# Half-width cluster choice in the opening, products summed in PSUM in the later first layers, and late weight sums on VectorE in a fused attention and MLP kernel

## The chip, the cores and the metric

The kernel runs on one core of a Trainium2 chip. The metric is the device time of one execution in microseconds (us). The core has a TensorE for matrix products (PE in the profile, with its weight loads apart as PEld), a VectorE (DVE), a ScalarE (ACT), a GpSimd (POOL) and a SyncE (SP), whose queue here issues nearly all DMAs. Each engine works through its own queue in order, and semaphores make one engine wait for another. SBUF is the on-chip memory of 128 partitions; PSUM is the small memory of eight banks that TensorE writes its products to and can add them up in.

## The reference, cut to what matters

```python
# attention: B=4, H=8 heads, S=768, D=64, 16 clusters
q_assign = argmax(q_n @ c_n^T)          # per head; k_assign alike
mask     = q_assign[:, None] == k_assign[None, :]
scores   = where(mask, q @ k^T / 8, -1e9)
attn     = softmax(scores)
x        = attn @ v                      # then (B, H, S, D) -> (3072, 512)
# MLP: w_in 512 x 2048, w_out 2048 x 512 (given as 64-bit floats)
h = x @ w_in
g = h / (1 + exp(-1.702 * h))
out = g @ w_out
```

A query attends only to the keys of its own cluster. All sums are made in fp32. The weights come as 64-bit floats, and the kernel rounds them to 32 bits itself.

## The kernel before, in words

**Attention.** Two heads form a pair, and there are 16 pairs. A pair is worked in 12 units: two halves of the queries, six tiles of 128 keys each. The loop over `t` does two units per turn. For a unit, `scores` makes the transposed scores (keys on partitions, 384 queries along the row) in PSUM, `part` adds the mask as a second product into the same bank, `exps` takes the exponential on ScalarE, `add_up` adds the exponentials into the denominators (on GpSimd, in halves of 384; the first sum of every even group on VectorE), and one turn later `values` multiplies with v. After every third turn `row_sums_of` sums over the partitions with a product, and `normalise` divides on VectorE.

The mask of the first pair is made from one-hot rows: `prep_turn` transposes q and k of pair 0 with TensorE, `prep_near` scores them against the centroids, `prep_assign` finds the best centroid on VectorE and writes a one-hot tile `hot`, and `prep_hot` transposes it into `hots0` and `hots1`, which `part` multiplies. The later pairs go through two rows of codes in DRAM instead (`prep_spread`). The preparation of pair p + 1 is spread over the turns of pair p.

`rounding` converts one chunk of 512 weights per partition, in five steps on VectorE, with the help of a PSUM bank. There are 32 chunks. `step` does one step, and a list of turns says where five steps (a whole chunk) are done. A chunk also issues the load of the chunk two places on. `keep_busy(n)` issues n products of an identity matrix that nobody reads (fillers) into the tile `idle`.

**MLP.** For each of the four batches a first and a second layer follow. The first layer is cut into 2x2 blocks and uses seven products per block of outputs in place of eight. `first7` does this for one of eight values of `f`: each product is a pair of contractions of 128 into a PSUM bank, and VectorE adds of a bank and the tile `G` combine the products (seven adds, one copy on ScalarE). `finish` is the activation, on ScalarE. The operands of the products are sums of blocks of x (`sums_x`, tiles Tx2 to Tx4, on VectorE) and of w_in (`sums_w`, on GpSimd).

The second layer uses two levels of this, 49 products in seven steps `k`: `second49(k, ...)` does the seven products of one step and already adds products up in PSUM banks x and v. Its operands are sums of G (`sums_t`, `sums_G`, on VectorE, in tiles E0 to E2, Tx2 to Tx4, Y and G itself) and sums of w_out (tile Wz, three per step). In batch 0 `keep_w` makes the Wz sums on GpSimd and stores them in DRAM, and the later batches load them. Those of steps 5 and 6 are made late, inside the second layer of batch 0, by `load_sums(k, made=True)`. After each step the result is added into the Y tiles, on GpSimd except for steps 4 and 5 (`i in (5, 7)`) of the last batch. While a second layer runs, VectorE also makes the next batch's `sums_x` and turns finished outputs for their stores (`store`).

The order of each queue is the order in which the program is written (manual scheduling): nothing is moved by a scheduler.

Of the kernel before, what the change touches and what calls it, by code (L numbers as in the profile page):

```python
# [8 lines left out]
FP32 = mybir.dt.float32  # L9
# [29 lines left out]
def fast(  # L39
# [31 lines left out]
    P = 128  # L71
# [44 lines left out]
    def short():  # L116
        return tmp.tile([P, HALF], FP32, name="short")
# [180 lines left out]
                rhs=ident_h[:, None, :].broadcast_to((P, 4, P)),  # L298
                start=True, stop=True)

    keep_busy(6)
    cps = bank()
    nc.tensor.transpose(out=cps[:, 0:P], in_=cc.rearrange("p a d -> p (a d)"),
                        identity=ident)
# [62 lines left out]

    def prep_assign(p):
        ps = bank()
        if p > 0:  # L370
            nc.vector.transpose(out=ps[:, 0:HALF], in_=sT.pop(p)[:, 0:HALF])
        else:
            for n in range(NH):
                nc.tensor.transpose(out=ps[:, n * P:(n + 1) * P],
                                    in_=sT[p][:, n * P:(n + 1) * P],
                                    identity=ident)
# [4 lines left out]
        eq = sc if p > 0 else short().bitcast(BF16)[:, 0:n * NC].rearrange(  # L381
            "p (n c) -> p n c", c=NC)
# [7 lines left out]
        if p == 0:  # L390
            code[p] = asg.tile([P, n], FP32, name="code", bufs=1)
            nc.vector.tensor_reduce(out=code[p], in_=eq, axis=AX.X,
                                    op=ALU.max)
            nc.vector.tensor_tensor(
                out=hot[:, :, 0:NC],
                in0=code[p][:, :, None].broadcast_to((P, n, NC)),
                in1=rank[:, None, :].broadcast_to((P, n, NC)),
                op=ALU.is_equal)
            return
        nc.vector.tensor_reduce(  # L400
            out=codes[:, 0:n].rearrange("p (w a j) -> p w j a", a=2, j=NJ),
            in_=eq.rearrange("p (w j a) c -> p w j a c", a=2, j=NJ),
            axis=AX.X, op=ALU.max)
        turned = ps[:, HALF:HALF + SQ]
        nc.vector.transpose(out=turned, in_=codes)
        row = code[p] = asg.tile([P, 2, SQ], BF16, name="row")
        nc.vector.tensor_copy(out=row[:, 0], in_=turned)
        nc.vector.scalar_tensor_tensor(
            out=row[:, 1], in0=turned, scalar=1.0 / CODE, in1=row[:, 0],
            op0=ALU.mult, op1=ALU.mult)  # L410
# [14 lines left out]
                    in_=line[b, at:at + NJ, :].rearrange(  # L425
                        "j t -> (j t)")[None, :])

    def prep_hot(p):


        rows = slice(0, 2 * SQ)
        for w in range(2):
            hots[w] = hp1.tile([P, S], BF16, name=f"hots{w}")
            ps = bank().bitcast(BF16)
            for h in range(2):
                for n in range(NH):
                    at = (h * NH + n) * P
                    nc.tensor.transpose(
                        out=ps[rows, at:at + P],
                        in_=hot_w(w, h, n), identity=ident_h)  # L440
            dst = hots[w][rows, :]
            if w == 0:
                nc.vector.tensor_copy(out=dst, in_=ps[rows, 0:S])
            else:
                nc.scalar.activation(out=dst, in_=ps[rows, 0:S], func=AF.Copy,
                                     scale=FAR, bias=-FAR)
# [6 lines left out]
    PREP += [prep_near, prep_assign,  # L453
             lambda p: (prep_hot if p == 0 else prep_spread)(p)]

# [202 lines left out]

    steps = (0, 0, 0, 5, 0, 5)
    made = sums_x(0)
    for p, i in [(0, i) for i in range(6)] + [(1, i) for i in range(2)]:
        prep(p, i)
        if p == 0 and i in (1, 3):
            load_w(i // 2)
        if (p, i) == (0, 4):
            keep_busy(3)
    for t in range(NT + 2):
        us = range(2 * t, 2 * t + 2) if t < NT else ()  # L670
        for u in us:
            scores(u)
        if t == 0:
            keep_busy(6)
            prep(0, 6)
            keep_busy(4)
        for u in us:
            part(u)
        for u in us:
            exps(u)  # L680
# [12 lines left out]
        while later:  # L693
            later.pop()()
        if 1 <= t <= NT:
            for u in range(2 * t - 2, 2 * t):
                values(u)
        if t >= 2 and (t - 2) % TG == TG - 1:
            row_sums_of((t - 2) // TG)
        while work and PREP[work[0][1]] == prep_near:  # L700
            prep(*work.pop(0))
        if t >= NT - 8 and t < NT:
            XT = list(next(made))
        for p, i in work:
            prep(p, i)
        for _ in range(0 if t in (0, 1, 2, NT - 1) else 5 if t == 4 else
                       steps[t % (2 * TG)]):
            step()
        if tests and t % (2 * TG) in (1, 2, 3, 5):
            tests.popleft()()  # L710
        if t >= 2 and (t - 2) % TG == TG - 1:
            normalise((t - 2) // TG)
# [70 lines left out]

    def spare_y():
# [62 lines left out]
    def first7(b, f, X, T):  # L847
# [31 lines left out]
        add(g1[:, 0], p, g1[:, 0])  # L879
        finish(g2[:, 0])  # L880
        finish(g1[:, 0])

    def after7(f):

# [142 lines left out]
    pend = iter(())  # L1027
    for b in range(B):
        for f in range(FB):
            first7(b, f, *XT)  # L1030
            sums_w(b * FB + f + 2)
            if f:
                after7(f - 1)
# [43 lines left out]
        for k in range(7):  # L1077
# [461 lines left out]
```

## Time and profile before

| | us |
|---|---|
| median of three runs | 901.17 (900.03 to 901.57) |
| the profiled execution's own time | 900.34 |
| span of its instructions | 898.5 |
| TensorE busy in the span | 885.8 |
| VectorE busy | 728.3 |
| GpSimd busy | 497.4 |
| ScalarE busy | 366.1 |

The span runs from the first to the last instruction that the profiler recorded; all positions below are microseconds from its start. By TensorE's timeline the first scores start at 11.44, attention ends at about 342, and then first and second layers alternate: 342 to 414 and 414 to 481 for batch 0, and so on to 891. A row of the profile names line, engine, operation, output and inputs, shape and count; what stands in brackets is the idle time of the engine just before and what ended it.

### The profile page before, as it was taken

How to read it: one execution, taken by the hardware profiler on the slowest of the kernel's cores; microseconds unless marked ns; L12 is line 12 of the kernel's file. 1: busy time of each engine (PE TensorE's matmuls, PEld its weight loads, DVE VectorE, ACT ScalarE, POOL GpSimd, SP SyncE). 2: the span in 40 equal slices, each digit the busy share in tenths (PEclk: the TensorE clock that was granted, in tenths of full speed). 3: DMA queues.
4: the chain of work that ended last, by engine and by line, in shares of the span. 5: the costliest groups of instructions: out<-in, count | busy, mean ns of one | idle time of the engine just before them, and what ended most of it. 6: DMA issues, size and time to landing. Idle time of an engine off the chain costs nothing.

```text
span 898.5 us, 17781 instructions
## 1 busy us (share of the span) xinstructions
PE 885.8 (99%) x6720; PEld 581.4 (65%) x6720; DVE 728.3 (81%) x1183; ACT 366.1 (41%) x819; POOL 497.4 (55%) x469
## 2 busy tenths in 40 slices
PE   8999999999999999999999999999999999999997
PEld 3444444444444445558996557998556998556996
DVE  4999989999999997998998556798556798556795
ACT  3677767777677764322111232111232111222111
POOL 5899999998999998693274221143121134120130
PEclk9999999999999999999999999999999999999999
DMA  9566556666575310036113202223202223200224
GB/s 175 122 129 112 103 120 130 143 143 133 133 139 119 85 43 19 0 122 230 71 54 107 52 1 71 84 74 107 53 1 70 73 76 117 43 10 0 71 71 109
DMA packets 176333, 78.97 MB, mean 88 GB/s; under 512 B 152824, under 2 KB 159472, under 8 KB 176240
## 3 DMA queue, kind: packets, MB, share of 16 engines
q1 hardware_dynamic: 175984, 77.63, 35.2%
q8 instruction: 55, 0.90, 0.4%
q14 instruction: 38, 0.31, 0.1%
q10 hardware_dynamic: 256, 0.13, 0.1%
HBM read 61.03 MB, written 16.70 MB: 87 GB/s over the span
## 4 chain that ended last, share of the span: by engine, by line
PE 87%; DVE 8%; issue 2%; POOL 1%; DMA 1%; ACT 0%; SPq 0%; DVEq 0%; ACTq 0%; POOLq 0%
PE b L854 32%; PE b L904 23%; PE s L472 13%; PE o L537 12%; PE s L495 3%; PE m L554 3%; DVE G L598 2%; DVE E L598 2%; POOL sum L521 1%; PE m L348 1%; DVE Tx L598 1%; DMA in<-in_k_dram 1%; DVE x L598 0%; DVE e L200 0%; DVE y L845 0%
## 5 line engine op out<-in xcount | busy, mean ns | idle before, releaser
L521 POOL TENSOR_TENSOR sum<-sum,A 128x384 f32<-128x384 f32 x252 | 265.5, 1091 | 25.7 <-ACT A L503 16.6
L845 DVE TENSOR_TENSOR G<-b,G 128x384 f32<-128x384 f32 x224 | 123.1, 556 | 98.7 <-PE b L854 89.5
L503 ACT ACTIVATE A<-s 128x768 f32<-128x768 f32 x192 | 146.3, 809 | 91.1 <-PE s L495 71.0
L598 POOL TENSOR_TENSOR Y<-y,Y 128x768 f32<-128x768 f32 x28 | 67.4, 2421 | 175.0 <-DVE y L845 151.0
L859 ACT ACTIVATE G<-G 128x384 f32<-128x384 f32 x128 | 66.3, 523 | 199.1 <-DVE G L845 197.7
L472 PE MATMUL s<-T,T 64*64 64x384 f32 x1536 | 142.9, 487 | 0.7 <-ACT A L503 0.7
L537 PE MATMUL o<-A,inv 64*64 64x384 f32 x1536 | 141.2, 483 | 0.0
L598 POOL TENSOR_TENSOR W<-w_in 128x256 f32<-128x256 f32 x32 | 23.6, 737 | 163.8 <-PE b L854 163.5
L598 DVE TENSOR_TENSOR G<-G 128x768 f32<-128x768 f32 (+1 forms) x92 | 104.5, 1159 | 0.0
L472 PEld LDWEIGHTS s<-T,T 64*64 64x64 f32 x1536 | 54.9, 132 | 70.1 <-ACT A L503 36.4
L854 PE MATMUL b<-x,W 128*128 128x384 f32 x256 | 93.1, 486 | 0.0
L854 PE MATMUL b<-Tx,w_in 128*128 128x384 f32 x256 | 93.1, 486 | 0.0
L854 PE MATMUL b<-x,w_in 128*128 128x384 f32 x256 | 88.6, 486 | 0.0
L537 PEld LDWEIGHTS o<-A,inv 64*64 64x64 f32 x1536 | 58.3, 133 | 38.5 <-issue 33.5
L854 PEld LDWEIGHTS b<-x,W 128*128 128x128 f32 x256 | 48.6, 190 | 33.9
L854 PEld LDWEIGHTS b<-Tx,w_in 128*128 128x128 f32 x256 | 48.6, 190 | 33.9
L854 PEld LDWEIGHTS b<-x,w_in 128*128 128x128 f32 x256 | 48.5, 190 | 33.5 <-issue 0.6
L904 PE MATMUL b<-G,w_out 128*128 128x192 f32 x320 | 55.9, 326 | 0.0
L904 PEld LDWEIGHTS b<-G,w_out 128*128 128x128 f32 x320 | 52.7, 190 | 1.1
L904 PE MATMUL b<-E,Wz 128*128 128x192 f32 x288 | 51.5, 328 | 1.4 <-DVE E L598 1.4
L904 PEld LDWEIGHTS b<-E,Wz 128*128 128x128 f32 x288 | 47.1, 190 | 3.4 <-POOL Wz L598 1.3
L854 PE MATMUL b<-Tx,W 128*128 128x384 f32 x128 | 46.6, 487 | 1.5 <-DVE Tx L598 1.5
(169 smaller groups left out, 1366.4 us busy)
## 6 DMA issues: line engine op xcount, KB each, us to landing
Wz<-kept_w SPq DMA_DIRECT2D x78, 256.0 KB
raw<-in_moe_w_in_dram SPq DMA_DIRECT2D x16, 512.0 KB
raw<-in_moe_w_out_dram SPq DMA_DIRECT2D x16, 512.0 KB
inv<-in_v_dram SPq DMA_DIRECT2D x16, 384.0 KB
in<-in_q_dram SPq DMA_DIRECT2D x60, 96.0 KB
in<-in_k_dram SPq DMA_DIRECT2D x60, 96.0 KB
kept<-x SPq DMA_DIRECT2D x24, 192.0 KB
x<-kept SPq DMA_DIRECT2D x24, 192.0 KB
```

What stands on the lines that cost most here:

```text
L348: nc.tensor.matmul(out=ps[r:r + SQ, w * NJ * SQ:(w + 1) * NJ * SQ] .rearrange("p (j t) -> p j t", t=SQ), lhsT=cT[:, p % HP].rearrange("p a ...
L472: nc.tensor.matmul(out=ps[c:c + D, a, 0:HALF], lhsT=T[p, 1][rows, kt * P + c:kt * P + c + D], rhs=T[p, 0][rows, h * HALF:(h + 1) * HALF], ...
L495: nc.tensor.matmul(out=s_of[u][c:c + D, a, :], lhsT=rows_of[1, p % 2][rows, kt * P + c:kt * P + c + D], rhs=rows_of[0, p % 2][rows, h * HA ...
L503: nc.scalar.activation(out=A_of[u], in_=s_of.pop(u), func=AF.Exp, scale=SCALE)
L521: nc.gpsimd.tensor_tensor(out=sum_of[g][:, a], in0=(A_of[u - 1] if kt == 1 else sum_of[g])[:, a], in1=A_of[u][:, a], op=ALU.add)
L537: nc.tensor.matmul(out=o_of[g][a * D:(a + 1) * D, r, 0:HALF], lhsT=v_in[p][rows, a, kt, :], rhs=A[rows, a, :], start=(kt == 0), stop=(kt = ...
L554: nc.tensor.matmul(out=ps[a * D:(a + 1) * D, 0:HALF], lhsT=twos, rhs=sm[:, a, :], start=(i == 0), stop=(i == len(parts) - 1))
L598: engine.tensor_tensor(out=o, in0=a, in1=b, op=(ALU.add if op == "+" else ALU.subtract))
L845: nc.vector.tensor_tensor(out=o, in0=p, in1=a, op=ALU.add)
L854: nc.tensor.matmul(out=ps[:, 0:HALF], lhsT=a[:, c], rhs=x(c), start=(c == 0), stop=(c == 1))
L859: nc.scalar.activation(out=g, in_=g, func=AF.Gelu_apprx_sigmoid, scale=2.0)
L904: nc.tensor.matmul(out=ps, lhsT=A[n][:, f], rhs=M[n][:, f], start=start and f == 0, stop=(f == FQ - 1), skip_group_check=True)
```

## The change

It has four parts.

- **The opening.** `prep_assign` and `prep_hot` of pair 0 become two halves of the tokens: `first_turns` does the transposes, the generator `choice(h)` does the five VectorE operations for one half, and `prep_hot(h)` transposes one half and copies it into half of `hots0` and `hots1`. For w = 0 the transposes go to the second bank of `idle`. Unit 2 gets its `part` and `exps` ahead of the scores of unit 3, and the second half of the one-hot work stands between them. The q and k turns of pair 1 on VectorE come after the second half's choice. The fillers change from 6, 3, 6 and 4 to 8, 2, 1, 3 and 3, the last three behind the first `part`.
- **The rounding chunks.** Turn t = 5 does none any more, and turn t = 91 (NT - 5), in the last pair, does one.
- **PSUM sums.** For batches 1 to 3 a new `first7_psum` takes the place of `first7`. It uses three banks per f, lets TensorE add four of the seven products into them, and leaves three VectorE adds and three ScalarE copies. One activation reads PSUM directly.
- **Late sums on VectorE.** The Wz sums made inside batch 0's second layer, and the Y sums of steps 4 and 5 of batch 0, go to VectorE.

```diff
-    keep_busy(6)
+    keep_busy(8)
...
+    def first_turns(p):
+        first.append(bank())
+        for n in range(NH):
+            nc.tensor.transpose(out=first[0][:, n * P:(n + 1) * P], in_=sT[p][:, n * P:(n + 1) * P], identity=ident)
...
+    def choice(h):
+        n = NJ * 2
+        ps, eq = first
...
+        nc.vector.tensor_reduce(out=best.rearrange("p (n a) -> p n a", a=2), in_=sc, axis=AX.X, op=ALU.max)
+        yield
+        nc.vector.tensor_tensor(out=eq4, in0=sc, in1=..., op=ALU.is_equal)
+        nc.vector.tensor_tensor(out=eq[:, h], in0=eq[:, h], in1=ranks, op=ALU.mult)
+        nc.vector.tensor_reduce(out=of, in_=eq[:, h], axis=AX.X, op=ALU.max)
+        nc.vector.tensor_tensor(out=hot..., in0=of..., in1=rank..., op=ALU.is_equal)
+        yield
...
+    def prep_hot(h):
+        rows, cols = slice(0, 2 * SQ), slice(h * HALF, (h + 1) * HALF)
+        pss = idle[:, 1, :].bitcast(BF16), bank().bitcast(BF16)
+        for w in (1, 0):
+            for n in range(NH):
+                nc.tensor.transpose(out=pss[w][rows, n * P:(n + 1) * P], in_=hot_w(w, h, n), identity=ident_h)
+        nc.scalar.activation(out=hots[1][rows, cols], in_=pss[1][rows, 0:HALF], func=AF.Copy, scale=FAR, bias=-FAR)
+        nc.vector.tensor_copy(out=hots[0][rows, cols], in_=pss[0][rows, 0:HALF])
...
         if (p, i) == (0, 4):
-            keep_busy(3)
+            keep_busy(2)
+    halves = [choice(h) for h in range(2)]
+    for h in (0, 0, 1):
+        next(halves[h])
     for t in range(NT + 2):
...
             scores(u)
+            if u == 2:
+                part(u)
+                exps(u)
+                prep_hot(1)
         if t == 0:
-            keep_busy(6)
-            prep(0, 6)
-            keep_busy(4)
+            keep_busy(1)
+            prep_hot(0)
+            keep_busy(3)
+            next(halves[1])
+            for i in range(2):
+                prep(1, i)
         for u in us:
-            part(u)
+            if u != 2:
+                part(u)
+        if t == 0:
+            keep_busy(3)
...
-        for _ in range(0 if t in (0, 1, 2, NT - 1) else 5 if t == 4 else
-                       steps[t % (2 * TG)]):
+        for _ in range(0 if t in (0, 1, 2, 5, NT - 1) else
+                       5 if t in (4, NT - 5) else steps[t % (2 * TG)]):
             step()
...
-    def keep_w(k, o):
+    def keep_w(k, o, engine=nc.gpsimd):
...
-            sums(nc.gpsimd, ((o, x, op, z),))
+            sums(engine, ((o, x, op, z),))
...
-            keep_w(k, [W[k][:, i] for i in range(3)])
+            keep_w(k, [W[k][:, i] for i in range(3)], nc.vector)
...
+    def first7_psum(b, f, X, T):
...
+        g1, g2 = G[:, f], G[:, f + FB]
+        x, z, v = (bank_b() for _ in range(3))
+        product(x, A_in(0, 0, f), lambda c: X[0, 0, c])
+        nc.scalar.copy(g1[:, 0], x)
+        product(z, A_in(0, 1, f), lambda c: X[1, 0, c])
+        add(g1[:, 0], z, g1[:, 0])
+        product(x, S[2], lambda c: T[2, c], False)
+        nc.scalar.copy(g1[:, 1], x)
+        finish(g1[:, 0])
+        product(v, S[1], lambda c: T[1, c])
+        nc.scalar.copy(g2[:, 1], v)
+        product(x, S[3], lambda c: T[3, c], False)
+        add(g2[:, 1], x, g2[:, 1])
+        finish(g2[:, 1])
+        product(v, S[4], lambda c: X[1, 1, c], False)
+        add(g1[:, 1], v, g1[:, 1])
+        finish(g1[:, 1])
+        product(x, A_in(1, 1, f), lambda c: T[4, c], False)
+        finish(g2[:, 0], x)
...
-            first7(b, f, *XT)
+            (first7_psum if b else first7)(b, f, *XT)
...
-            second49(k, extra, final)
+            second49(k, extra, b in (0, B - 1))
```

More of the change, by code (lines that the diff above doesn't have):

```diff
@@ L369, in prep_assign @@
         ps = bank()
[L370 to L376, printed above, removed]
+        nc.vector.transpose(out=ps[:, 0:HALF], in_=sT.pop(p)[:, 0:HALF])
         n = NJ * 4
@@ L380, in prep_assign @@
         nc.vector.tensor_reduce(out=best, in_=sc, axis=AX.X, op=ALU.max)
-        eq = sc if p > 0 else short().bitcast(BF16)[:, 0:n * NC].rearrange(
-            "p (n c) -> p n c", c=NC)
+        eq = sc
         nc.vector.tensor_tensor(
@@ L388, in prep_assign @@
             op=ALU.mult)
[L390 to L399, printed above, removed]
         nc.vector.tensor_reduce(
@@ L426, in prep_spread @@
                         "j t -> (j t)")[None, :])
-    def prep_hot(p):
-        rows = slice(0, 2 * SQ)
+    def first_turns(p):
+        first.append(bank())
+        for n in range(NH):
+            nc.tensor.transpose(out=first[0][:, n * P:(n + 1) * P],
+                                in_=sT[p][:, n * P:(n + 1) * P],
+                                identity=ident)
+        first.append(short().bitcast(BF16)[:, 0:HALF].rearrange(
+            "p (h n c) -> p h n c", h=2, c=NC))
         for w in range(2):
@@ L433, in prep_hot @@
             hots[w] = hp1.tile([P, S], BF16, name=f"hots{w}")
[L434 to L446, printed above, removed]
+    first = []
@@ new lines, in choice @@
+    def choice(h):
+        n = NJ * 2
+        ps, eq = first
+        sc = ps[:, 0:HALF].rearrange("p (n h x) -> p n h x", h=2, x=2 * NC)[
+            :, :, h].rearrange("p n (a c) -> p n a c", c=NC)
+        eq4 = eq[:, h].rearrange("p (n a) c -> p n a c", a=2)
+        best = asg.tile([P, n], FP32, name="best0", bufs=2)
+        nc.vector.tensor_reduce(out=best.rearrange("p (n a) -> p n a", a=2),
+                                in_=sc, axis=AX.X, op=ALU.max)
+        yield
+        nc.vector.tensor_tensor(
+            out=eq4, in0=sc,
+            in1=best.rearrange("p (n a) -> p n a", a=2)[
+                :, :, :, None].broadcast_to((P, NJ, 2, NC)),
+            op=ALU.is_equal)
+        ranks = rank[:, None, :].broadcast_to((P, n, NC))
+        nc.vector.tensor_tensor(out=eq[:, h], in0=eq[:, h], in1=ranks,
+                                op=ALU.mult)
+        of = asg.tile([P, n], FP32, name="code0", bufs=2)
+        nc.vector.tensor_reduce(out=of, in_=eq[:, h], axis=AX.X, op=ALU.max)
+        nc.vector.tensor_tensor(
+            out=hot.rearrange("p (n h a) c -> p n h a c", h=2, a=2)[
+                :, :, h, :, 0:NC],
+            in0=of.rearrange("p (n a) -> p n a", a=2)[
+                :, :, :, None].broadcast_to((P, NJ, 2, NC)),
+            in1=rank[:, None, None, :].broadcast_to((P, NJ, 2, NC)),
+            op=ALU.is_equal)
+        yield
@@ new lines, in prep_hot @@
+    def prep_hot(h):
[3 more added lines that the diff above has]
+            for n in range(NH):
+                nc.tensor.transpose(out=pss[w][rows, n * P:(n + 1) * P],
+                                    in_=hot_w(w, h, n), identity=ident_h)
+        nc.scalar.activation(out=hots[1][rows, cols], in_=pss[1][rows, 0:HALF],
+                             func=AF.Copy, scale=FAR, bias=-FAR)
+        nc.vector.tensor_copy(out=hots[0][rows, cols],
+                              in_=pss[0][rows, 0:HALF])
@@ L452, in fast @@
     PREP = [lambda p, i=i: prep_turn(p, i) for i in range(4)]
[L453 to L454 removed]
+    PREP += [prep_near, lambda p: (prep_assign if p else first_turns)(p),
+             prep_spread]
     NG = 2 * NPAIR
@@ L662, in fast @@
     made = sums_x(0)
-    for p, i in [(0, i) for i in range(6)] + [(1, i) for i in range(2)]:
+    for p, i in [(0, i) for i in range(6)]:
         prep(p, i)
@@ L672, in fast @@
             scores(u)
+            if u == 2:
+                part(u)
+                exps(u)
+                prep_hot(1)
         if t == 0:
-            keep_busy(6)
-            prep(0, 6)
-            keep_busy(4)
+            keep_busy(1)
[4 more added lines that the diff above has]
+                prep(1, i)
         for u in us:
-            part(u)
+            if u != 2:
+                part(u)
+        if t == 0:
+            keep_busy(3)
         for u in us:
-            exps(u)
+            if u != 2:
+                exps(u)
         if recs:
@@ L881, in first7, with product, bank_b, finish @@
         finish(g1[:, 0])
+    def first7_psum(b, f, X, T):
+        S = w_of.pop(b * FB + f)
+        def product(ps, a, x, start=True):
+            for c in range(2):
+                nc.tensor.matmul(out=ps, lhsT=a[:, c], rhs=x(c),
+                                 start=start and c == 0, stop=(c == 1),
+                                 skip_group_check=True)
+        def bank_b():
+            return ps_b.tile([P, 512], FP32, name="b")[:, 0:HALF]
+        def finish(g, ps=None):
+            nc.scalar.activation(out=g, in_=g if ps is None else ps,
+                                 func=AF.Gelu_apprx_sigmoid, scale=2.0)
+        g1, g2 = G[:, f], G[:, f + FB]
[17 more added lines that the diff above has]
+        finish(g2[:, 0], x)
     def after7(f):
```

## The prediction

> **What bounds the kernel now.** I read the page first, then the busy table by stage, then TensorE's timeline where its idle is not nought, then the engine that ends each of those waits.
>
> ```profile
> PE 885.8 (99%) x6720; PEld 581.4 (65%) x6720; DVE 728.3 (81%) x1183; ACT 366.1 (41%) x819; POOL 497.4 (55%) x469
> ```
>
> TensorE (PE) is busy for all but 12.7 of 898.5 us, and no edit here takes a needed matmul away. So the change can only win TensorE's waits, or the time in which it is busy with fillers or at half speed. The table (stretch, then busy us of PE, PEld, DVE, ACT, POOL) says where those are:
>
> ```profile
> core 0: us, PE busy (x) PEld busy (x) DVE busy (x) ACT busy (x) POOL busy (x), PEclk, DMA share, GB/s
> ...
> 11.44:21.50 10.06, 9.32 (x96) 3.60 (x95) 5.74 (x9) 3.83 (x5) 3.35 (x5) 1.00 1.17 200
> ...
> 414.33:480.68 66.35, 64.90 (x394) 63.56 (x393) 60.63 (x72) 12.23 (x37) 28.66 (x14) 1.00 0.30 106
> 480.68:554.67 73.99, 72.50 (x225) 42.47 (x225) 44.35 (x86) 20.01 (x39) 18.62 (x25) 1.00 0.16 43
> 554.67:618.63 63.96, 63.96 (x394) 63.67 (x392) 58.04 (x76) 11.40 (x36) 19.16 (x8) 1.00 0.28 87
> 618.63:690.87 72.24, 72.24 (x226) 42.56 (x225) 40.69 (x81) 20.02 (x39) 17.15 (x24) 1.00 0.17 44
> ```
>
> The same second layer takes 66.35 us for batch 0 and 63.96 for batch 1, the same first layer 73.99 for batch 1 and 72.24 for batch 2. Batch 0's tail is 2.39 + 1.75 = 4.14 us above its twins. Later first layers have no idle at all.
>
> ```profile
> 1.63 2.74 PE L296 MATMUL o<-ident_h 128*128 128x512 bf16 x6 [1.63 <-DVE ident_h L250]
> 5.18 0.45 PE L303 MATMUL m<-ident,short 128*128 128x128 f32 x1 [0.81 <-DVE cT L291]
> ...
> 12.89 1.47 PE L296 MATMUL o<-ident_h 128*128 128x512 bf16 x6
> ...
> 16.08 0.50 PE L486 MATMUL s<-hots,hots 16*128 16x384 bf16 x4
> ...
> 19.26 1.52 PE L537 MATMUL o<-A,inv 64*64 64x384 f32 x16
> ...
> 21.50 1.52 PE L472 MATMUL s<-T,T 64*64 64x384 f32 x16
> ...
> 61.34 1.77 PE L554 MATMUL m<-sum,twos 128*64 128x384 f32 x4
> ...
> 465.08 1.54 PE L904 MATMUL b<-E,Wz 128*128 128x192 f32 x8 [0.67 <-DVE E L598]
> ...
> 475.40 1.54 PE L904 MATMUL b<-E,Wz 128*128 128x192 f32 x8 [0.68 <-DVE E L598]
> ...
> 483.62 1.56 PE L854 MATMUL b<-Tx,W 128*128 128x384 f32 x4 [1.49 <-DVE Tx L598]
> ```
>
> Columns: start, length, instruction, idle before and its releaser. Three things: six fillers take 2.74 us at the start and 1.47 at 12.89; the row sum at 61.34 lasts 1.77 where its like lasts 0.87; three waits in batch 0 end on VectorE.
>
> ```profile
> 459.03 1.75 DVE L598 TENSOR_TENSOR G<-G 128x768 f32<-128x768 f32 x1
> ...
> 469.51 2.45 DVE L598 TENSOR_TENSOR E<-G 128x768 f32<-128x768 f32 x1
> ...
> 599.30 0.94 DVE L598 TENSOR_TENSOR G<-G 128x768 f32<-128x768 f32 x1
> 600.28 0.96 DVE L598 TENSOR_TENSOR Tx<-G 128x768 f32<-128x768 f32 x1
> ```
>
> The first and third rows are the same instruction of batches 0 and 1: 1.75 us while GpSimd makes the Wz sums, 0.94 while it is idle. GpSimd at work on SBUF nearly doubles the time of VectorE's SBUF sums.
>
> ```profile
> 43.26 8.06 POOL L521 TENSOR_TENSOR sum<-sum,A 128x384 f32<-128x384 f32 x8 [4.05 <-DVE sum L514]
> ...
> 58.80 3.41 POOL sum L521 x3
> ```
>
> The second is from the chain of waits: GpSimd's sums end last before the row sum at 61.34, and they are late because at 39.2 GpSimd sat 4.05 us waiting for VectorE's sum, queued behind three rounding chunks.
>
> **The change part by part.**
>
> *Opening, work.* The choice of cluster was five operations, 11.55 to 14.27, 2.72 us. The first half needs five of half width. No such row; the nearest is the 128x192 add of L845, 0.35 us, with 0.03 between: 4 x 0.385 + 0.27 for the bf16 one = 1.81. Gain 0.91. From there to the first `part` was 1.81 us (12 transposes, 0.80 on ScalarE). Now 6 transposes to their landing 0.6, copies of half size (0.48 by L339 on ScalarE, 0.3 on VectorE) end at 1.0; but the first of the next three fillers waits for VectorE's copy, since both lie in the tile `idle`, and the three (0.22 each at full speed) stand ahead of `part`: 1.7. Gain 0.1. From `part` to `values` was 19.26 - 16.08 = 3.18. Now ScalarE runs exps of unit 2 and the second half of `hots1` before `part` of unit 3: exps 0 ends at +1.2, scores and `part` of 2 to +2.2, exps to +3.2, copy to +3.6, `part` to +3.9. Loss 0.7. The other fillers lie in such waits. VectorE's extra 0.9 us of halves lies in its idle 1.5 before 18.00. Net 0.3 earlier at 21.50, between -0.2 and 0.6.
>
> *Opening, clock.* The row PEclk says full speed throughout. Yet fillers follow one another at 0.43 us from 1.63 and at 0.22 from 10.3; the near scores at 9.4 last 0.67 us and at 9.91 0.49. So full speed came at about 9.5. [...] Eight fillers end at 1.63 + 8 x 0.43 = 5.05 and close the 0.81 us gap before 5.18[...]. Keys land at 7.3; from there to ScalarE's copy at 10.43 is 3.1 us: two half-turns (0.75 each, 0.4 warm) and the last near score (1.0, 0.5 warm) with ScalarE copies of 0.48 between; warm about 2.1. By PEclk the gain is 0[...]. I take 0.9: spacing is measured, PEclk doesn't show it.
>
> *Rounding chunk.* The one at t = 5 held VectorE 36.92 to 40.45. Without it the sum behind it starts 3.5 us sooner, GpSimd is bound by ScalarE's exps again, and 61.34 loses its excess: 0.9. The chunk returns at t = 91, where one costs 331.07 to 335.20 = 4.1 us. VectorE has one idle of 2.8 us there; its last sum for batch 0 (Tx4) slips from 339.3 to 343.4 and is wanted at 348.5. GpSimd, working without a break to 341.1, is slowed by it: 0 to -1.0, I take -0.3. Later weight loads move with their chunks on SP, and the next k loads no longer stand behind one that waited for ScalarE. Nothing waits for them.
>
> *Late sums.* VectorE gains 6 Wz sums of 128x512 (0.65 each, between L204's 0.69 and the 128x768 sums' 0.95) and 4 Y sums (0.9 each, batch 3's row): 7.5 us. It loses GpSimd's interference. Queue from 458.84: three Wz to 460.8, y, G, Tx3 to 462.95 (wanted 462.8: TensorE waits 0.3), E1 464.1, transposes, y, E2 466.2, two Y, three Wz to 469.9, y, G, E0 472.0 (wanted 472.2), E1 473.2 (473.6), E2 475.3 (477.5), x sums 476.3, Y 478.1, Tx2 479.8. Seven steps of 9.1 from 423.76 end step 6 at 478.36, so 478.7 with the wait, against 480.68: 2.0. Tx2, wanted at 481.3 as the third product now comes first to need it, is ready: 1.65 more. Sum 3.65. If Wz costs 1.3 as under interference, Tx3 and all behind it come 2 us later: the low end is 0.8. SP's stores of these sums now wait for VectorE; behind them stand a turned output and the next Wz loads, wanted at 554. Cover enough.
>
> *PSUM sums, three first layers.* Fourteen matmul pairs per f stay. Seven VectorE adds (0.56) become three, ScalarE copies go from one to three. There is no idle to win inside. [...] But another product (1.29 us) lies between in each case, leaving 0.5 to 0.6 spare, and `second49` already accumulates after ScalarE's copy in 63.96 us without idle. I take 0. What it does win: VectorE reaches the next layer's first E sums about 1 us sooner; the second product group there starts 0.26 late now (63.96 against 7 x 9.1). Three batches: 0.8, between 0 and 0.8.
>
> Sum: 0.3 + 0.9 + 0.9 - 0.3 + 3.65 + 0.8 = 6.25 us. The profiled execution took 900.34 (span 898.5 and 1.8 around it): 894.1. The median of the three runs is 0.83 above it: 894.9. I say 894.6.
>
> **The rivals.**
> 1. The opening and the end give little: [...]fillers ahead of `part` charged, GpSimd late at the end. Then 0.3 + 0 + 0.7 - 1.0 + 3.65 + 0.6 = 4.25: 896.5. For it: fillers sit on the path. Against: the cold spacing.
> 2. VectorE becomes the bound in batch 0's second layer: 60.6 busy of 66.35 already, and 7.5 more. Then 0.8 in place of 3.65: 3.4, 897.4. Against: batch 1's VectorE rows without GpSimd.
> 3. Slower: the hand-over before the last product, which waits for VectorE's add with only 0.5 spare. If adds come late by more (a transposed store or G sum ahead of them), each of 24 passes stalls. From 0.26 us a pass it eats the gain, from 0.34 the kernel is slower by over 0.2%; with 0.6 it is 909. Against: those operations stand behind the third add, with 3 us before the next is due.
>
> **How the numbers follow.** Forecast 0.66, rival 1 0.2, rival 2 0.1, rival 3 0.04. The range 892.9 to 897.6 takes in the first three with run noise (1.5 us between the three runs). About 0.2% (1.8 us) is what a measurement of this kernel can tell from no change. Faster 0.94, same 0.03, slower 0.03.
>
> **What would show it.** Second layer of batch 0 near 64.3 and first layer of batch 1 near 72.3; fillers at 0.43 giving way to full spacing before the keys' turn; scores of t = 2 near 20.3; the row sum of t = 13 at 0.87; VectorE's E sums at 0.95 in steps 4 and 5. I am wrong if TensorE shows waits on ScalarE or VectorE inside `first7_psum`, or if the E waits of batch 0 are still there.

## The result and the profile after

The changed kernel takes 898.33 us (median of 14 runs, 896.51 to 899.77) against 900.46 for the kernel before (also 14 runs). The ratio is 0.9976, with a 95% interval of 0.9967 to 0.9984: 2.1 us faster. The forecast was 894.6 with a range of 892.9 to 897.6, so the direction was right and the size was not. The profiled execution of the changed kernel took 899.77 us, the slowest of the 14, with a span of 897.7.

First the totals (busy time of each engine, from the page of the changed kernel):

```profile
PE 885.6 (99%) x6718; PEld 582.4 (65%) x6718; DVE 677.0 (75%) x1103; ACT 385.9 (43%) x868; POOL 478.9 (53%) x459
```

TensorE is as busy as before (885.8). VectorE lost 51 us of work and GpSimd 18, and neither shows in the time one for one. Next the busy table by stage of the changed kernel: opening, second layer of batch 0, first and second layer of batch 1, first layer of batch 2.

```profile
10.65:20.50 9.85, 9.25 (x92) 3.47 (x91) 6.38 (x15) 3.98 (x6) 5.46 (x7) 1.00 1.25 201
417.95:482.31 64.36, 64.20 (x393) 63.64 (x392) 58.58 (x86) 12.19 (x37) 9.88 (x4) 1.00 0.34 111
482.31:554.55 72.24, 72.24 (x226) 42.60 (x225) 27.74 (x53) 26.62 (x55) 17.34 (x23) 1.00 0.17 46
554.55:618.33 63.78, 63.78 (x393) 63.67 (x392) 58.06 (x76) 11.36 (x36) 22.41 (x10) 1.00 0.29 85
618.33:690.62 72.29, 72.29 (x226) 42.50 (x225) 26.47 (x50) 26.64 (x55) 17.34 (x23) 1.00 0.17 46
```

The second layer of batch 0 went from 66.35 to 64.36 us and the first layer of batch 1 from 73.99 to 72.24. All that was forecast of batch 0 is there. The loss is in the last pair of the attention. TensorE's timeline of the changed kernel (start, length, instruction, idle before and its releaser):

```profile
1.63 3.59 PE L296 MATMUL o<-ident_h 128*128 128x512 bf16 x8 [1.63 <-DVE ident_h L250]
...
5.36 2.84 PE L334 MATMUL m<-ident,in 128*128 128x128 f32 x12
8.13 1.47 PE L360 MATMUL m<-T,cT 128*32 128x384 f32 x8
...
20.50 1.52 PE L492 MATMUL s<-T,T 64*64 64x384 f32 x16
...
60.24 0.87 PE L574 MATMUL m<-sum,twos 128*64 128x384 f32 x4
...
332.41 2.84 PE L492 MATMUL s<-T,T 64*64 64x384 f32 x16 [3.44 <-ACT A L523]
335.02 0.86 PE L515 MATMUL s<-rows,rows 64*64 64x384 bf16 x8
335.66 2.77 PE L557 MATMUL o<-A,inv 64*64 64x384 f32 x16
338.37 0.87 PE L574 MATMUL m<-sum,twos 128*64 128x384 f32 x4
...
345.60 1.56 PE L888 MATMUL b<-x,w_in 128*128 128x384 f32 x4
```

The scores of t = 2 start at 20.50 (21.50 before), and the row sum of t = 13 lasts 0.87 in place of 1.77. At 332.41 stands something that the prediction does not have: TensorE idle for 3.44 us, and behind it the same matmuls at half their pace (2.84 and 2.77 us for what takes 1.47 elsewhere). The same changed kernel on VectorE and then on ScalarE shows what TensorE waited for:

```profile
324.57 0.68 DVE L189 TENSOR_SCALAR m<-raw 128x512 int32<-128x512 int32 x1
...
328.02 0.76 DVE L207 TENSOR_TENSOR w_out<-m,e 128x256 f32<-128x256 f32 x2
328.69 0.57 DVE L584 STREAM_TRANSPOSE short<-m 128x384 f32<-128x384 f32 x1
...
329.56 0.59 DVE L589 STREAM_TRANSPOSE m<-few 128x384 f32<-128x384 f32 x1
```

```profile
330.19 0.21 ACT L609 ACTIVATE few<-few 128x12 f32<-128x12 f32 x1 [4.02 <-DVE m L589]
...
331.57 1.48 ACT L523 ACTIVATE A<-s 128x768 f32<-128x768 f32 x2
```

`check` is a pair of small ScalarE operations (L609 and L611). It works in place on the reciprocals in the tile `few`, so it has to wait until `normalise` has read them.

Read it from the end. TensorE has no PSUM bank for the scores of turn 94 until ScalarE has taken the exponentials of turn 93 (331.57). In ScalarE's queue these stand behind the `check` of turn 91's denominator (L609), which waits 4.02 us for the `normalise` of turn 91 on VectorE (L584 to L589). In VectorE's queue that `normalise` stands behind the rounding chunk that the change put into turn 91 (324.57 to 328.69).

The clock shows in the busy table of the changed kernel, cut finely there (the columns behind the five engines are granted clock, DMA share and GB/s):

```profile
325.88:328.97 3.09, 3.09 (x44) 1.32 (x36) 2.99 (x6) 0.29 (x1) 3.09 (x4) 1.00 0.00 0
328.97:332.41 3.44, 0.00 (x1) 0.01 (x1) 3.34 (x7) 2.19 (x8) 3.05 (x3) 0.86 0.00 0
331.00:331.50 0.50, 0.00 (x0) 0.00 (x0) 0.47 (x2) 0.50 (x2) 0.50 (x1) 0.97 0.00 0
331.50:332.00 0.50, 0.00 (x0) 0.00 (x0) 0.50 (x2) 0.50 (x3) 0.50 (x1) 0.50 0.00 0
332.41:335.66 3.25, 3.25 (x24) 1.40 (x28) 3.15 (x6) 2.05 (x5) 1.96 (x2) 0.50 0.19 66
335.66:338.37 2.71, 2.71 (x21) 0.73 (x13) 1.25 (x4) 1.51 (x2) 1.75 (x2) 0.51 0.00 0
338.37:345.60 7.23, 7.23 (x76) 2.95 (x72) 3.42 (x6) 4.26 (x12) 7.00 (x9) 1.00 0.07 27
```

The third and fourth rows cut the end of the wait finer. The granted clock falls at about 331.47, 2.5 us after TensorE's last product, while TensorE still waits, and it is back at about 338.3. From 332.41 to 338.37 are 5.96 us; the same sequence, from scores to row sum, took 3.01 in turn 91. So the stretch costs 3.44 for the wait and 2.95 for the clock. The two sums around it are shorter than before (the row sum of turn 91 by 0.67, the last one by 0.38), which is most of why the whole pair loses 5.5 and not 6.4.

### The profile page after: what moved, and what is told of

Same layout as the page of the kernel before. It is cut to its first block, busy times and chain, and to the rows that moved or that the text cites. A ratio compares the mean times of both kernels' runs of the same rounds, so it can differ in the third digit from the quotient of the medians.

```text
span 897.7 us, 17708 instructions
## 1 busy us (share of the span) xinstructions
PE 885.6 (99%) x6718; PEld 582.4 (65%) x6718; DVE 677.0 (75%) x1103; ACT 385.9 (43%) x868; POOL 478.9 (53%) x459
## 4 chain that ended last, share of the span: by engine, by line
PE 95%; DVE 3%; issue 0%; ACT 0%; POOL 0%; ACTq 0%; POOLq 0%; DVEq 0%
PE b L975 28%; PE b L923 24%; PE s L492 13%; PE o L557 13%; PE b L888 8%; PE s L515 3%; PE m L574 3%; PE m L348 1%; PE o L296 1%; DVE e L200 0%; PE s L506 0%; DVE x L595 0%; DVE m L193 0%; DVE e L196 0%; PE m L334 0%
## 5 line engine op out<-in xcount | busy, mean ns | idle before, releaser
L879 DVE TENSOR_TENSOR G<-b,G 128x384 f32<-128x384 f32 x128 | 69.6, 556 | 142.3 <-PE b L923 136.2
L618 POOL TENSOR_TENSOR Y<-y,Y 128x768 f32<-128x768 f32 x24 | 59.9, 2506 | 163.7 <-DVE y L879 136.5
L923 PE MATMUL b<-Tx,w_in 128*128 128x384 f32 x192 | 69.9, 487 | 0.0
L923 PE MATMUL b<-x,W 128*128 128x384 f32 x192 | 69.8, 486 | 0.0
L923 PE MATMUL b<-x,w_in 128*128 128x384 f32 x192 | 65.9, 486 | 0.0
L931 ACT ACTIVATE G<-G 128x384 f32<-128x384 f32 x72 | 37.7, 524 | 52.1 <-DVE G L879 52.1
L923 PEld LDWEIGHTS b<-Tx,w_in 128*128 128x128 f32 x192 | 36.3, 190 | 25.7 <-DVE G L879 0.8
L923 PEld LDWEIGHTS b<-x,W 128*128 128x128 f32 x192 | 36.5, 190 | 25.4
L923 PEld LDWEIGHTS b<-x,w_in 128*128 128x128 f32 x192 | 36.4, 190 | 24.6
L515 PE MATMUL s<-rows,rows 64*64 64x384 bf16 x720 | 46.0, 325 | 0.0
```

Source lines behind the costliest of these rows:

```text
L515: nc.tensor.matmul(out=s_of[u][c:c + D, a, :], lhsT=rows_of[1, p % 2][rows, kt * P + c:kt * P + c + D], rhs=rows_of[0, p % 2][rows, h * HA ...
L618: engine.tensor_tensor(out=o, in0=a, in1=b, op=(ALU.add if op == "+" else ALU.subtract))
L879: nc.vector.tensor_tensor(out=o, in0=p, in1=a, op=ALU.add)
L923: nc.tensor.matmul(out=ps, lhsT=a[:, c], rhs=x(c), start=start and c == 0, stop=(c == 1), skip_group_check=True)
L931: nc.scalar.activation(out=g, in_=g if ps is None else ps, func=AF.Gelu_apprx_sigmoid, scale=2.0)
```

## The experiments

Theory 1 is the chain just read: chunk, `normalise`, `check`, exponentials, scores. Theory 2: VectorE's chunk slows GpSimd's sums, which hold the buffers of the exponentials, so that a chunk costs as much anywhere in the last pair.

**The chunk behind the normalise.**

```diff
-                       5 if t in (4, NT - 5) else steps[t % (2 * TG)]):
+                       5 if t in (4,) else steps[t % (2 * TG)]):
...
             normalise((t - 2) // TG)
+        if t == NT - 5:
+            for _ in range(5):
+                step()
```

> The changed kernel with one edit: in turn 91 the rounding chunk stands behind the normalise of that turn on VectorE, not ahead of it. Same work. Theory 1 (order in the queues: ScalarE's check of the denominators waits for VectorE's normalise, which stands behind the 4.1 us chunk, and the exponentials of turn 93 stand behind that check, so TensorE has no bank for the scores of turn 94): TensorE's 3.44 us wait at 328.97 is gone, so are the half-speed matmuls behind it, and the time is 4 to 6 us below the changed kernel: 892.5 to 894.3. Theory 2 (the chunk slows GpSimd's sums, which hold the buffers of the exponentials, wherever in the last pair it stands): the wait stays at 2.5 us or more and the time is 897 to 899.

Measured: 896.13 us, ratio to before 0.9965 (0.9951 to 0.9978). The wait at 329 and the half speed are gone, as theory 1 says, but the time is not as low as I expected. TensorE's timeline of this run has two smaller losses in the last pair:

```profile
322.43 1.74 PE L574 MATMUL m<-sum,twos 128*64 128x384 f32 x4
...
341.46 1.56 PE L891 MATMUL b<-x,w_in 128*128 128x384 f32 x4 [0.98 <-ACT short L566]
```

The first, 0.87 us too long, lies ahead of the chunk (327.70) and cannot come from it: GpSimd worked from 315.63 without a break and was late, as in the kernel before, where the like row lasts 1.62. The second is the same chain once more. The backlog on VectorE makes the `normalise` of turn 94 late, ScalarE's `check` waits 2.08 us for it (L609 at 339.18), and the copy that frees a bank for the first layer stands behind that check.

**The check one turn later.**

```diff
-        if recs:
+        if recs and t != NT - 4:
             check(*recs)
```

> The changed kernel with the chunk left ahead of the normalise in turn 91, but ScalarE's check of that denominator is issued one turn later, behind the exponentials of turn 93. Theory 1 (ScalarE's queue carries the wait to TensorE): the exponentials no longer stand behind a wait for VectorE, TensorE's wait is below 0.5 us, time 892.5 to 894.5. If VectorE's lateness reaches TensorE in another way (row sums' bank, x tiles) or theory 2 holds: wait above 2 us, time 897 to 899.

Measured: 896.78 us, ratio 0.9969 (0.9957 to 0.9981). TensorE's waits:

```profile
331.87 1.52 PE L557 MATMUL o<-A,inv 64*64 64x384 f32 x16 [1.15 <-ACT short L566]
...
342.19 1.56 PE L888 MATMUL b<-x,w_in 128*128 128x384 f32 x4 [1.57 <-ACT short L566]
```

VectorE's chunk is as early and its `normalise` as late as in the changed kernel, but the wait of 3.44 us and the half speed are gone. So ScalarE's place in the chain is shown. What stands behind the postponed check now waits: a copy of ScalarE, which `values` needs (1.15 us). The second wait is the one of the run above: the `check` of turn 94's denominator waits 2.50 us for a late `normalise`, and a copy stands behind it. 896.78 is above the 892.5 to 894.5 that I expected, since both waits together are 2.7 us.

**Unread products in the wait,** to part the wait from the clock.

```diff
         us = range(2 * t, 2 * t + 2) if t < NT else ()
+        if t == NT - 2:
+            spare = bank()
+            for _ in range(14):
+                nc.tensor.matmul(
+                    out=spare, lhsT=ident_h,
+                    rhs=ident_h[:, None, :].broadcast_to((P, 4, P)),
+                    start=True, stop=True)
```

> The changed kernel with 14 unread products (0.216 us each, 3.0 us) put ahead of the scores of turn 94, in a spare PSUM bank, so that they lie inside TensorE's 3.44 us wait. It separates the wait from the clock that falls after it. If the half speed behind the wait (scores, part and values take 6.0 us in place of 3.0) is caused by TensorE's idleness: the matmuls behind the wait are at full spacing, idle is about 0.4 us, and the time is 1.3 to 3.0 us below the changed kernel, 895.3 to 897. If the clock falls for another reason: no change, 897.5 to 899.

Measured: 900.07 us, ratio 1.0007 (0.9997 to 1.0017). The experiment missed its aim. In the profiled execution its products waited 1.99 us for VectorE themselves (for L596, the end of the late `normalise`, whose bank they had been given), started at 331.04, and then stood 3.18 us long ahead of the scores. So it does not part the wait from the clock. The record holds a hint that such a shorter wait can be followed by half speed too: eight of the 13 executions have a mean granted clock of 0.998 and take 898.98 to 900.35 us, five have 0.996 or 0.997 and take 901.25 to 902.30. The one trace is of the first kind and has no half speed, so this is not shown. The next one has the same 14 products at the end of turn 93, ahead of that turn's chunk, and so gets another bank:

```diff
+        if t == NT - 3:
+            spare = bank()
+            for _ in range(14):
+                nc.tensor.matmul(
+                    out=spare, lhsT=ident_h,
+                    rhs=ident_h[:, None, :].broadcast_to((P, 4, P)),
+                    start=True, stop=True)
         for _ in range(0 if t in (0, 1, 2, 5, NT - 1) else
```

> The changed kernel again with 14 unread products inside TensorE's wait, but with their bank taken in turn 93, so that it is the bank of the chunk of turn 91 (free at 328.7) and not that of the normalise. They should start as TensorE comes to them, at about 329, and end by 332. If the half speed behind the wait comes from TensorE's idleness: no clock below 0.998, full spacing behind the wait, 895.5 to 897.3. If not: 897.5 to 899, with half-speed matmuls behind the fillers.

Measured: 897.40 us, ratio 0.9968 (0.9956 to 0.9980), 0.9 below the changed kernel. TensorE:

```profile
328.07 1.47 PE L557 MATMUL o<-A,inv 64*64 64x384 f32 x16
329.47 3.20 PE L743 MATMUL m<-ident_h 128*128 128x512 bf16 x14
332.60 1.52 PE L492 MATMUL s<-T,T 64*64 64x384 f32 x16
333.94 0.50 PE L515 MATMUL s<-rows,rows 64*64 64x384 bf16 x8
334.26 1.47 PE L557 MATMUL o<-A,inv 64*64 64x384 f32 x16
335.67 0.87 PE L574 MATMUL m<-sum,twos 128*64 128x384 f32 x4
```

The scores start as late as before, and everything behind them runs at full pace: 3.07 us from the scores to the row sum in place of 5.96. So TensorE's idleness causes the half speed here; in the profiled execution of the changed kernel that is 2.9 us. The medians are only 0.9 apart, and the two intervals overlap, since the clock seems not to fall in every execution of the changed kernel. Eight of the 14 have a mean granted clock of 0.995 to 0.997 and a median of 898.74 us; six have 0.998 or 0.999 and a median of 897.57, which as a ratio to before (0.9968) is that of the kernel with the fillers, whose six executions all have 0.998 or more. This is a hint and no proof: the clock also falls behind the last product, while the last stores run (3.1 us behind it in the changed kernel, 5.1 in the kernel before), and one run whose timeline shows no half pace behind the opening has a mean of 0.997 all the same (the late sums on GpSimd, below).

**The chunk where it was, at turn 5.**

```diff
-        for _ in range(0 if t in (0, 1, 2, 5, NT - 1) else
-                       5 if t in (4, NT - 5) else steps[t % (2 * TG)]):
+        for _ in range(0 if t in (0, 1, 2, NT - 1) else
+                       5 if t == 4 else steps[t % (2 * TG)]):
```

> The changed kernel with the rounding chunk put back at turn 5, where the kernel before has it, and none in turn 91; the other three parts of the change stay. Theory 1: no wait at 329, and the 0.9 us at the row sum of turn 13 come back; 893.3 to 895.0, that is 0.5 to 1.0 above the kernel with the chunk behind the normalise. If the chunk's place is worth less than I think: 896 to 898.

Measured: 895.62 us, ratio 0.9959 (0.9945 to 0.9973). Without its moved chunk the change brings 4.1 parts in a thousand rather than 2.4. I had expected this one to be 0.5 to 1.0 us above the chunk behind the `normalise`; it is 0.5 below. The two intervals do not part them, but the other one does keep its two losses in the last pair. Its own loss at turn 13 is there: from that row sum to the next are 11.37 us, as in the kernel before (11.36), against 10.46 in the changed kernel.

**The moved chunk alone, in the kernel before.**

```diff
-        for _ in range(0 if t in (0, 1, 2, NT - 1) else 5 if t == 4 else
-                       steps[t % (2 * TG)]):
+        for _ in range(0 if t in (0, 1, 2, 5, NT - 1) else
+                       5 if t in (4, NT - 5) else steps[t % (2 * TG)]):
```

> The kernel before with one part of the change alone: the rounding chunk goes from turn 5 to turn 91. Theory 1 (chunk ahead of normalise, ScalarE's check behind it, exponentials behind that): the row sum of turn 13 loses its 0.9 us excess, and in the last pair TensorE waits about 3.4 us before the scores of turn 94, in some executions with a half-speed stretch behind it: 1.5 to 3.5 us slower than before, 901 to 903. If the wait needs the other parts of the change: within 1 us of before, 899 to 900.5.

Measured: 903.68 us, ratio 1.0034 (1.0022 to 1.0047): 3.3 us slower than before, just above the 901 to 903 us that I expected. TensorE's and ScalarE's lines are those of the changed kernel:

```profile
333.22 2.61 PE L472 MATMUL s<-T,T 64*64 64x384 f32 x16 [3.44 <-ACT A L503]
```

```profile
331.00 0.21 ACT L589 ACTIVATE few<-few 128x12 f32<-128x12 f32 x1 [4.02 <-DVE m L569]
```

The row sum of t = 13 is at its short length here too (the stage from the row sum of t = 10 to that of t = 13 lasts 9.68, and the next begins 10.45 later in place of 11.36). So this part gains 0.9 us early and loses 4.3 late (27.71 us before from the row sum of t = 88 to the first layer, 32.04 here); it needs none of the other parts for either.

**The chunk at turn 95,** behind VectorE's last sum for batch 0.

```diff
-        for _ in range(0 if t in (0, 1, 2, 5, NT - 1) else
-                       5 if t in (4, NT - 5) else steps[t % (2 * TG)]):
+        for _ in range(0 if t in (0, 1, 2, 5) else
+                       5 if t in (4, NT - 1) else steps[t % (2 * TG)]):
```

> The changed kernel with the chunk of turn 91 moved to turn 95, the last one, where VectorE has an idle stretch of 2.8 us and no normalise of its own; none in turns 5 and 91. Theory 1: both costs are gone (0.9 at the row sum of turn 13, the wait in the last pair); about 1 us better than with the chunk at turn 5: 894.0 to 895.2. If a chunk anywhere in the last pair holds up ScalarE's check and with it the copies that the first layer waits for: first layer 1 to 2 us late, 895.5 to 897.5.

Measured: 894.67 us, ratio 0.9937 (0.9923 to 0.9950). It beats the kernel before by 5.7 us and has the lowest median of all runs. VectorE around the chunk:

```profile
336.41 0.78 DVE L618 TENSOR_TENSOR Tx<-x,Tx 128x384 f32<-128x384 f32 x1
337.12 0.68 DVE L189 TENSOR_SCALAR m<-raw 128x512 int32<-128x512 int32 x1
...
340.30 0.76 DVE L207 TENSOR_TENSOR w_out<-m,e 128x256 f32<-128x256 f32 x2
340.97 0.57 DVE L584 STREAM_TRANSPOSE short<-m 128x384 f32<-128x384 f32 x1
```

The chunk fills the idle stretch that the prediction had seen, and the last `normalise` behind it is one for which no copy or exponential of the attention waits. From the row sum of t = 88 to the first layer are 27.60 us (27.71 before), and TensorE is not idle in them. Theory 2 falls: the same work in the same pair costs nothing at this place, and in the first experiment, behind the `normalise` of the same turn, it did not bring the wait at 329 either.

**The other terms, one at a time.** With the chunk at turn 5, the late Wz and Y sums go back to GpSimd:

```diff
-            keep_w(k, [W[k][:, i] for i in range(3)], nc.vector)
+            keep_w(k, [W[k][:, i] for i in range(3)])
...
-            second49(k, extra, b in (0, B - 1))
+            second49(k, extra, b == B - 1)
```

> The changed kernel with the chunk at turn 5 and with the late Wz and Y sums of batch 0 back on GpSimd. The prediction's term for the late sums is 3.65 us. If it is right: second layer of batch 0 at 66.3 us and first layer of batch 1 at 73.5 to 74.0, 3.3 to 4.0 us above the kernel with the chunk at turn 5: 898.9 to 899.7. If the PSUM first layer of batch 1 already gives part of it (its first product doesn't need Tx2): first layer of batch 1 at 72.3 to 73 and 897.3 to 898.8.

Measured: 899.02 us, ratio 0.9986 (0.9978 to 0.9993). TensorE's waits of batch 0 are back:

```profile
465.80 1.54 PE L975 MATMUL b<-E,Wz 128*128 128x192 f32 x8 [0.67 <-DVE E L618]
...
476.11 1.54 PE L975 MATMUL b<-E,Wz 128*128 128x192 f32 x8 [0.68 <-DVE E L618]
...
484.42 1.53 PE L923 MATMUL b<-Tx,W 128*128 128x384 f32 x4 [0.30 <-DVE Tx L618]
```

The second layer of batch 0 takes 66.31 us and the first layer of batch 1 73.10, which is 1.93 and 0.86 above the kernel with the chunk at turn 5. So taking the late sums back loses 2.8 of the 3.74 us won there. The other 0.9 stays with `first7_psum`, whose third product and not its second asks for Tx2. It is not a gain on top of the late sums: the run without `first7_psum` below has 64.27 and 72.24 us in these two layers, so with the late sums on VectorE the first layer of batch 1 is as short without it.

With the chunk at turn 95, only the Wz sums go back to GpSimd (the first of the two edits above):

> The kernel with the chunk at turn 95, with the late Wz sums of batch 0 back on GpSimd and the Y sums left on VectorE. If GpSimd's Wz work slows VectorE's sums of steps 4 and 5 (the prediction's reading): both waits for E of 0.67 us are back (spacing gaps of 1.0 each), second layer of batch 0 at 66.0 to 66.6, first layer of batch 1 at 72.24 to 72.6, 896.3 to 897.1. If the Y sums are the ones that slow VectorE: second layer at 64.4 to 65, 894.6 to 895.3.

Measured: 896.52 us, ratio 0.9960 (0.9946 to 0.9974); second layer of batch 0 66.18 us, first layer of batch 1 72.24. VectorE's first E sum of step 4 and TensorE's wait for it:

```profile
462.50 2.02 DVE L618 TENSOR_TENSOR E<-G,Tx 128x768 f32<-128x768 f32 x1
```

```profile
464.66 1.54 PE L975 MATMUL b<-E,Wz 128*128 128x192 f32 x8 [1.74 <-DVE E L618]
```

The time is as I expected, but it is lost in one wait of 1.74 us and not in two of 0.67: without the Y sums GpSimd makes all six Wz sums in a row (456.50 to 466.87), beside VectorE's sums of step 4. These take 1.75 to 2.06 us where they are 128x768, and in the changed kernel, with the Wz sums on VectorE, 0.94 to 0.96: here GpSimd's Wz sums slow VectorE's. With the Y sums left on VectorE the wait for Tx2 did not come back.

With the chunk at turn 95, `first7` in place of `first7_psum`:

```diff
-            (first7_psum if b else first7)(b, f, *XT)
+            first7(b, f, *XT)
```

> The kernel with the chunk at turn 95 (894.67 us), with first7 in place of first7_psum in batches 1 to 3. The prediction gave the PSUM sums 0.8 us in all, from the start of the next second layer; the runs so far show 0.18 us per second layer (63.78 against 63.96). If that is all: second layers of batches 1 to 3 at 63.96, first layer of batch 1 at 72.24 to 72.5, 895.0 to 895.6. If the order of the products matters too (first7 needs Tx2 for its second product, 1.3 us earlier): first layer of batch 1 up to 1 us longer, 895.6 to 896.6. If the PSUM sums cost something inside: 894.0 to 894.6.

Measured: 895.36 us, ratio 0.9948 (0.9934 to 0.9961). The second layers are at 63.96, 63.96 and 64.07 again, as before the change, where `first7_psum` has 63.78, 63.77 and 63.82; first layers are at 72.24, where two of the three had 72.29. In the trace the PSUM sums are worth 0.5 us; the medians, 0.7 apart, do not part the two kernels beyond their intervals.

The fillers of the opening: 6 at the start in place of 8, and in the other kernel none behind the first `part`, both with the chunk at turn 95.

```diff
-    keep_busy(8)
+    keep_busy(6)
```

> The kernel with the chunk at turn 95, with 6 unread products at the start in place of 8. The prediction gave 0.9 us to the earlier full clock that 8 are to bring. If it is so: the transposes of k and the near scores are at half spacing again, first scores 0.7 to 1.0 us later, 895.3 to 895.8. [...]

Measured: 895.06 us, ratio 0.9946 (0.9932 to 0.9959). TensorE of this run:

```profile
5.17 0.45 PE L303 MATMUL m<-ident,short 128*128 128x128 f32 x1 [0.80 <-DVE cT L291]
...
7.41 1.51 PE L334 MATMUL m<-ident,in 128*128 128x128 f32 x6 [0.28 <-DMA in<-in_k_dram]
8.86 1.53 PE L360 MATMUL m<-T,cT 128*32 128x384 f32 x8
...
11.43 1.52 PE L492 MATMUL s<-T,T 64*64 64x384 f32 x16
```

The gap of 0.80 is back, the transposes of k take 1.51 us at half pace (0.85 in the kernel with 8), and the first scores start at 11.43. In the eleven kernels with 8 fillers they start between 10.07 and 10.77, in the two others with 6 (the kernel before, and that with the chunk moved) at 11.44 and 11.09. So the trace shows the clock term. The medians, 895.06 and 894.67, differ by less than their spread, and 895.06 lies 0.2 below the 895.3 to 895.8 that I expected.

```diff
-        if t == 0:
-            keep_busy(3)
```

> The kernel with the chunk at turn 95, without the three unread products behind the first part (0.65 us of TensorE time). If they only fill a wait for the exponentials: 894.4 to 894.9, TensorE idle where they were. If they hold back the scores of unit 2: 0.3 to 0.6 us faster, 894.0 to 894.4. If they keep the clock up: half spacing somewhere before 20 us and 895 or more.

Measured: 894.79 us, ratio 0.9946 (0.9932 to 0.9960), so the fillers lie in a wait, and no cost or gain of theirs can be seen. TensorE of this run is idle where they were:

```profile
15.39 0.88 PE L492 MATMUL s<-T,T 64*64 64x384 f32 x8 [0.74 <-ACT A L523]
```

## Why the prediction was wrong in size, and what of it held

The terms of the sum, each measured between the same two instructions in the profiled executions before and after:

| term | predicted gain, us | measured |
|---|---|---|
| opening, work and clock (scores of t = 2) | 0.3 + 0.9 | 1.00 |
| chunk gone from turn 5 (from there to the scores of t = 14) | 0.9 | 1.00 |
| chunk in the last pair | -0.3, bound -1.0 | -5.5 |
| late sums of batch 0 (66.35 to 64.36, 73.99 to 72.24) | 3.65 | 3.74 |
| PSUM sums, batches 1 to 3 | 0.8 | 0.52 |

The row of the last pair runs from the row sum of t = 88 to the first layer: 314.27 to 341.98 is 27.71 us before, 312.38 to 345.60 is 33.22 after. With another 0.11 lost in between, the transposes of the last store start 0.64 earlier (891.14 to 890.50). The forecast for everything else was within 0.3 us, term by term: 6.55 us in all, and 6.26 measured. That is not luck in the opening: the first scores start 0.79 earlier (clock; the 0.9 forecast was my estimate, and the trace of before did not show that eight fillers would bring the full pace forward), the first `part` comes 0.95 sooner behind them (forecast 0.91 + 0.1), and from there to `values` it takes 0.75 longer (forecast 0.7). It is not luck in the second layer of batch 0 either: counted from the layer's start, Tx3 and the last E sum of step 4 end at 48.6 and 51.7 us, where the prediction's queue had 48.6 and 51.9. Three slips in its working change little: six steps of 9.1 us, not seven, lead from 423.76 to 478.36; 462.95 against 462.8 is a wait of 0.15 and not of 0.3 (0.16 us of the layer are idle in the trace); and no reason stands for taking 894.6 where the sum gives 894.9.

**The step that failed** is the second half of the rounding chunk: "VectorE has one idle of 2.8 us there; its last sum for batch 0 (Tx4) slips" and "GpSimd ... is slowed by it: 0 to -1.0, I take -0.3". It counted who waits for VectorE's sums, and left out the next thing on VectorE's queue in the same turn, the `normalise`, with ScalarE's check behind it. The idle of 2.8 us was real, but it began at 339.3, 13 us behind the place of the `normalise` of turn 91 (326.27). The rows that give the price were in the trace of before (VectorE, then ScalarE):

```profile
327.14 0.59 DVE L569 STREAM_TRANSPOSE m<-few 128x384 f32<-128x384 f32 x1
```

```profile
327.22 1.51 ACT L503 ACTIVATE A<-s 128x768 f32<-128x768 f32 x2 [1.05 <-PE s L495]
328.62 0.21 ACT L589 ACTIVATE few<-few 128x12 f32<-128x12 f32 x1
```

VectorE's part is done at 327.73, and ScalarE comes to the check at 328.62 without having waited: 0.9 us of slack, against a chunk of 4.1. That makes the check 3.2 us late. In the two runs with unread products, where the row sum of turn 91 is late (1.50 and 1.51 us long) as in the kernel before (1.62), ScalarE waited 3.16 us for the `normalise`. In the changed kernel that row sum lasts 0.95, ScalarE comes to the check sooner, with a slack of about 0.1 by the same working, and it waited 4.02, TensorE 3.44.

**The second half of the price** is the clock. The prediction looked at the clock in the opening alone and did not ask what a new wait of over 3 us would set off. In the profiled execution of the changed kernel the clock fell to 0.50 after 2.5 us of an idle of 3.44 us, and the matmuls behind it took 2.84 and 2.77 us in place of 1.47. The waits of 1.15 to 1.99 us in the other profiled executions (1.15 and 1.57 with the check one turn later, 1.74 with only the Wz sums on GpSimd, 1.99 with the unread products) left no half-speed stretch.

The rivals: VectorE did not become the bound in batch 0 (its sums are at 0.95 us, and the waits for E are gone). No hand-over stall appears in `first7_psum`: in the first layers of batches 1 and 2 TensorE is busy for 72.24 of 72.24 and 72.29 of 72.29 us. The 0.5 us to spare that the prediction gives is an estimate, and the trace of before bears it out: one product lies between two uses of a bank, products follow one another at 1.29 us, and VectorE's add begins 0.20 us behind its product and takes 0.56. "GpSimd late at the end" was in rival 1, which put the pair at -1.0 in place of -0.3, but that is not the mechanism that took 5.5. With the chunk out of the way of the `normalise`, at turn 95, the whole change gives 894.67 us.

What stays open: the place of the chunk costs 5.6 us in the profiled execution (33.22 against 27.60 with the chunk at turn 95), but 3.5 between the two ratios (0.0039 of 900). The profiled execution is 1.4 us above the median of its kernel, and the six executions with the higher mean clock are 1.2 below the other eight, so executions without a fall of the clock probably explain the larger part; how much of the rest is the spread of the opening and of the final stores was not measured.

## What to carry to other kernels

A block moved into a queue is priced by what stands behind it in the same turn: follow each such instruction to the small bookkeeping operations on other engines and to what is queued behind those, and subtract the slack that the trace shows. An idle stretch of an engine pays only if the block stands in it, not if it lies in the same stage. And a new TensorE wait of about 2.5 us or more, after which the clock fell in the changed kernel, should be costed twice, once as a wait (3.44 us there) and once as the half speed that may follow (2.95).

## What the hardware showed that I had not expected

- The same idle of 3.44 us did not cost the same. In the changed kernel the clock fell 2.5 us after the last product and stayed at 0.50 for 6.8 us, which cost 2.95 us. In the kernel before with the chunk moved, scores to row sum took 4.76 us in place of 3.0, which cost about 1.75. By the lengths of its matmuls (scores 2.61 us, where 1.47 is full pace and 2.84 half; values 1.82, where those are 1.47 and 2.77) I estimate that TensorE had just begun again when the clock fell, and that it stayed down for about 3.5 us.
- Behind the last product TensorE has no more work, and the clock falls there too: 3.1 us after the product in the changed kernel's profiled execution, 5.1 in that of the kernel before. With the 2.5 us above, the idle ahead of a fall differs from place to place and from run to run, so a wait of 3.4 us might be followed by half speed in one execution and not in the next; no trace shows one that was not.
- The granted clock in the busy table shows that fall, but gave 1.00 for 1.63 to 5.12, where fillers follow one another at 0.43 us, twice the 0.22 of later ones. The slow start is read here from the spacing, not from that column.
- With the same eight fillers, full pace came by about 5 us in some profiled executions (the kernel with the chunk at turn 95, where the product of L303 at 5.02 takes 0.27 us) and only at about 7.6 in others (the changed kernel, where that product takes 0.45 and the transposes follow one another at 0.21 to 0.24 us before 7.2 and at 0.11 to 0.17 behind 7.65). The first scores start between 10.07 and 10.77 in these runs, to which the landing of the keys adds its own spread: the transposes that wait for it start at 6.73 with the chunk at turn 95 and at 7.11 in the run without the fillers behind the first `part`.
